# Rows turned later, their router product in the second value visit, their sums in the visit of step 8

## The chip, the cores and the metric

One core of a Trainium2 chip runs the whole program. The metric is the time of one execution on the device, in microseconds; several executions of a kernel are given by their median. The core has a matrix engine (TensorE, "PE" in the profile, its weight loads "PEld"), a vector engine (VectorE, "DVE"), an activation engine (ScalarE, "ACT"), a general one (GpSimd, "POOL"), and SyncE ("SP"), from whose queue nearly all transfers are issued. Each engine works through its own instructions in the order in which the program lists them. TensorE writes to PSUM alone; VectorE and ScalarE read from there.

## The reference, cut to what matters

Three stages, one after the other, all in float32:

```python
p_packed = sm_attn(p, k, v)                    # 8 batches x 8 heads, 32 packed queries over 576 keys
attn_out = sm_attn(q, p_packed, p_packed)      # 576 queries over the 32 packed rows
x = attn_out.transpose(0, 2, 1, 3).reshape(4608, 512)
h = x @ w_in;  x = (h * sigmoid(h)) @ w_out    # 512 -> 2048 -> 512
logits = x @ w_gate;  e_idx = argmax(logits, axis=1)          # 8 experts
gate_w = softmax(logits)[e_idx];  eom = sigmoid(x @ w_output_gate)[e_idx]
for e in range(8):                             # each row through its one expert
    out[mask] = gate_w * eom * (relu(x[mask] @ w1[e]) @ w2[e])
```

The router's logits (16 columns: 8 for the gate, 8 for the output gate) are needed for each of the 4608 rows before the rows can be sorted by expert.

## The kernel before, in words

**Batches and steps.** `batch(b)` runs for b = 0 to 7 (8 batches of 576 rows). Its loop over f, 16 passes, is called *steps* here. A step holds, in this order: `mm1` (12 products into the PSUM tile `ps_h`, which has one buffer and holds the hidden block f), `act` (ScalarE's tanh, then VectorE's multiplication that makes g; both read `ps_h`, so the next step's `mm1` waits for them), the side work of the first position (f, 0), the splitting of g into a high and a low half (ScalarE `ghi`, VectorE `glo`, and two small ones for the last 64 rows), whatever is in the list `late`, `mm2` of two steps ago (12 products, into four accumulators), and the side work of the second position (f, 1).

**Side work.** `extra_steps(b)` writes by hand which step and position each piece takes; pieces of one position run in the order in which they are entered. Three kinds are interleaved with batch b:
- the attention of batch b + 1, as `s1` to `s9`: `s1` scores of the packed queries (maxima on VectorE, then a copy `e` by ScalarE), `s2` their transposes, `s3` the products with the values, once for each of two halves r (step 5 for r = 0, step 7 for r = 1), which VectorE scales into `pp`; `s4` (step 8) transposes `pp` into `ppt`; `s5` scores of the queries, `s6` and `s7` their softmax, `s8` and `s9` (steps 11 and 14) its turn and its two halves;
- `step_m`, in every even step at the first position: it folds `ppt` into `w_in` (products, ScalarE's high half, VectorE's low half);
- the rows of batch b - 1, whose last `mm2` comes in step 1 of batch b.

**The rows.** A group has 4 blocks of 128 rows (after even batches) or 5 (after odd ones, with the rest of two batches). `regroup` (step 1) stores the rows to DRAM and loads them back in another order into `mid`; `row_x` turns one block within 32 by 32 squares on VectorE (line 296); `row_logits` multiplies with the router's weights, a fourth of the columns in each fourth of the partitions, and ScalarE copies the parts out; `row_sum` transposes the parts on TensorE, adds the fourths on VectorE, and goes on into `finish`: for each block a maximum and its index, then a few small operations. `finish` puts `pick` into `late`, which puts `weight` there a step later. `place` counts the rows of each expert with small products, and puts `put` into `late`, which computes each row's position and scatters the entries into the table `perm` by GpSimd, one call for each block.

**PSUM.** The accumulators take four banks, `ps_h` two. The other two are one tile "a" with one buffer: all of `s1` to `s5`, `step_m`, the rows and `place` use it in turn, and each new visit waits until the readers of the one before are done. `psum(b)` and `bank(...)` both hand it out.

In batch 7 there is no attention; its hook prepares the expert stage (copies and splits of expert weights, gathers of the first group's rows). `last_rows` and `experts` follow and use `row_logits`, `row_sum` and `place` for the last groups by themselves.

Of the kernel before, what the change touches and what calls it, by code (L numbers as in the profile page):

```python
# [21 lines left out]
DM = 512  # L22
# [13 lines left out]
NL = 2 * E8  # L36
# [48 lines left out]
class Kernel:  # L85
# [209 lines left out]
        xq, xt = [self.mid[:, g[n] + a * DM:g[n] + a * DM + DM] for n in ("xq", "xt")]  # L295
        self.nc.vector.transpose(out=xt.rearrange("p (t c j) -> p t c j", c=4, j=32), in_=xq.rearrange("p (t i c) -> p t c i", c=4, i=32))

    def row_logits(self, g, ps=None):
        n = g["n"]
        if ps is None:  # L300
            ps = self.bank("ps_rl")
        xt = self.mid[:, g["xt"]:g["xt"] + n * DM].rearrange("p (t c j) -> p c t j", c=4, j=32)
        if n == 1:
            xn = self.mid[:, g["xt"]:g["xt"] + DM]
            for c in range(4):
                self.nc.tensor.matmul(ps[:, 0, :NL], xn[:, c * 128:c * 128 + 128], self.wgt[:, c, :NL], start=(c == 0), stop=(c == 3))
            self.nc.vector.tensor_copy(out=g["lg"][:, 0, :], in_=ps[:, 0, :NL])
            self.finish(g)
            return
        for i, a in enumerate(range(0, n, 4)):  # L310
            m = min(n - a, 4)
            for c in range(4):
                self.nc.tensor.matmul(ps[32 * c:32 * c + 32, i, :m * 128], self.wgt[:, c, :], xt[:, c, 4 * a:4 * a + 4 * m, :], start=True, stop=True)
        part = self.mid[:, g["part"]:g["part"] + n * 128]
        self.nc.scalar.copy(out=part, in_=ps.rearrange("p a b -> p (a b)")[:, :n * 128])

    def row_sum(self, g):
        n, ps = g["n"], self.bank("ps_rs").rearrange("p a b -> p (a b)")
        for a in range(n):
            at = g["part"] + a * 128  # L320
            self.nc.tensor.transpose(ps[:, a * 128:a * 128 + 128], self.mid[:, at:at + 128], self.ident)
        self.nc.vector.tensor_reduce(out=g["lg"][:, :n, :], in_=ps[:, :n * 128].rearrange("p (a c m) -> p a m c", a=n, c=4)[:, :, :NL, :],
                                     axis=AX.X, op=ALU.add)
        self.finish(g)
# [107 lines left out]
    def extra_steps(self, b):  # L432
        sched = {}

        def at(f, pos, fn):
            sched.setdefault((f, pos), []).append(fn)

        if b + 1 < B:
            att = self.att_steps(b + 1)
            for f, pos, *step in ((0, 1, "s1", 0), (3, 1, "s1", 1), (4, 1, "s2", 0), (5, 1, "s3", 0), (6, 1, "s2", 1),  # L440
                                  (7, 1, "s3", 1), (8, 1, "s4"), (9, 1, "s5", 0), (10, 0, "s6", 0), (10, 1, "s7", 0),
                                  (11, 1, "s8", 0), (11, 1, "s9", 0), (12, 1, "s5", 1), (13, 0, "s6", 1), (13, 1, "s7", 1), (14, 1, "s8", 1), (14, 1, "s9", 1)):
                at(f, pos, att[tuple(step)])
            for f, what in ((0, "k1"), (3, "q0"), (5, "v1"), (9, "q1")):
                at(f, 1, lambda what=what: self.load_att(b + 1, what))
            at(14, 0, lambda: self.step_m(b + 1, 0))
        if b + 2 < B:
            for what in ("p", "k0", "v0"):
                at(13, 0, lambda what=what: self.load_att(b + 2, what))
        if b > 0:  # L450
            at(1, 1, lambda: self.regroup(self.group))
            for a in range(4 if b % 2 else 5):
                at(*((3, 0), (3, 1), (4, 0), (4, 1), (4, 1))[a], lambda a=a: self.row_x(self.group, a))
            if b + 1 == B:
                at(5, 1, lambda: self.row_logits(self.group))
            at(7, 0, lambda: self.row_sum(self.group))
            at(9, 0, lambda: self.place(self.group))
        for c in range(1, 8):
            at(2 * c - 2 + (b == 0 and (c == 1 or c % 2 == 0)), 0, lambda c=c: self.step_m(b, c))
        return sched  # L460
# [86 lines left out]
    def att_steps(self, b):  # L547
        nc, pa = self.nc, self.pa
# [35 lines left out]
        def s3(r):  # L584
            v = self.loads.pop((b, f"v{r}"))
            ps = self.psum(b)
            if r == 0 and b > 1:
                self.row_logits(self.group, ps)
            ps = ps[:, 1, 256:320]
            for ch in range(5):  # L590
                for c in range(4):
                    nc.tensor.matmul(ps[32 * c:32 * c + 32, :], a1[r][:, ch, 32 * c:32 * c + 32],
                                     v[:, ch, 64 * c:64 * c + 64], start=(ch == 0), stop=(ch == 4))
            nc.vector.tensor_scalar(out=self.pp[:, 64 * r:64 * r + 64], in0=ps,
                                    scalar1=st["sm"][:, 10 + r:11 + r], scalar2=None, op0=ALU.mult)

        def s4():
            ps = self.psum(b)
            nc.tensor.transpose(ps[:, 0, :128], self.pp, self.ident)
            ppt = self.p1.tile([128, 128], F32, tag="ppt", bufs=2, name="ppt")  # L600
            nc.scalar.copy(out=ppt, in_=ps[:, 0, :128])
            self.ppt[b] = ppt

        def grp(x):
            return x.rearrange("p a (t n) -> p (a t) n", n=NP)
# [34 lines left out]
        def s9(h):  # L640
# [3 lines left out]

        return {(f.__name__, *a): (lambda f=f, a=a: f(*a)) for f, a in
                [(f, (h,)) for f in (s1, s2, s3, s5, s6, s7, s8, s9) for h in range(2)] + [(s4, ())]}

    def step_m(self, b, c, split=False):
# [450 lines left out]
```

## Time and profile before

| | |
|---|---|
| median of 3 runs | 1237.77 us (1237.06 to 1238.42) |
| profiled execution | 1236.86 us, of which the span of instructions is 1235.0 |
| TensorE busy | 1171.0 us, 95% |
| its weight loads | 966.4 us, 78% |
| VectorE busy | 678.7 us, 55% |
| ScalarE busy | 467.4 us, 38% |
| GpSimd busy | 171.9 us, 14% |
| mean granted TensorE clock | 0.976 |
| DMA | 130.27 MB, mean 105 GB/s |

The span runs from the first instruction to the last; the time of the execution holds a little more around it. A matmul's end is modelled, so records of neighbours overlap, and a busy TensorE is not one at its peak. The granted clock is a share of the full 2.4 GHz; 0.5 is 1.2 GHz. In the rows below "[5.38 <-ACT e L561]" says that the engine stood idle for 5.38 us in front of this instruction, and that the instruction that ended the idle time was ScalarE's at line 561 on tile `e`.

### The profile page before, as it was taken

The page shows a single profiled execution, that of the slowest core. Times are in us where ns is not written, and L with a number is a line of the kernel's source. Part 1 is how long each engine was busy: PE and PEld are TensorE (multiplying, and loading weights), DVE is VectorE, ACT ScalarE, POOL GpSimd, SP SyncE. Part 2 cuts the span into 40 slices and gives each one's busy share as a digit, 9 for nine tenths or more (in the row PEclk, how much of TensorE's full clock was granted, in tenths as well). Part 3 has the DMA queues.
Part 4 walks back from the last instruction along what each step waited for, and adds up shares of the span by engine and source line. Part 5 has one row for each costly group of instructions (what it writes and reads, how often), then busy time and mean ns, then how long its engine had stood idle before and what let it go on. Part 6 is the DMA issues. An engine that isn't in the chain of part 4 may idle for free. (4 is left out here: it accounts for less than half of the span.)

```text
span 1235.0 us, 20793 instructions
## 1 busy us (share of the span) xinstructions
PE 1171.0 (95%) x8307; PEld 966.4 (78%) x8307; DVE 678.7 (55%) x1355; ACT 467.4 (38%) x913; POOL 171.9 (14%) x177
## 2 busy tenths in 40 slices
PE   7796989999989999989999989999999999999996
PEld 3575768778768777768777878879899998999985
DVE  6888646545646545645645746454454454544531
ACT  2343433433443433443433434323443434434331
POOL 0234201000001000000000121013312113111011
PEclk8699989999999999999999999999999999999999
DMA  8564230231240231131141052116645546455221
GB/s 321 177 208 171 95 77 24 95 71 44 62 107 25 76 91 44 45 104 45 61 105 35 9 144 71 69 45 205 188 110 180 150 132 197 115 176 162 70 74 41
DMA packets 105290, 130.27 MB, mean 105 GB/s; under 512 B 13888, under 2 KB 80640, under 8 KB 104928
## 3 DMA queue, kind: packets, MB, share of 16 engines
q1 hardware_dynamic: 97888, 108.76, 30.0%
q0 software_dynamic: 7296, 20.09, 5.0%
q8 instruction: 67, 1.10, 0.4%
q14 instruction: 39, 0.32, 0.1%
HBM read 99.12 MB, written 21.57 MB: 98 GB/s over the span
## 5 line engine op out<-in xcount | busy, mean ns | idle before, releaser
L728 PE MATMUL acc<-wo,ghi 128*128 128x512 f32 x1024 | 322.6, 397 | 0.0
L728 PEld LDWEIGHTS acc<-wo,ghi 128*128 128x128 f32 x1024 | 195.9, 191 | 38.8
L1013 PE MATMUL pu<-xt,w 128*128 128x256 f32 (+1 forms) x1536 | 214.5, 295 | 0.1
L677 PE MATMUL ps_h<-a,m_hi 128*128 128x288 f32 x1024 | 213.1, 301 | 0.6 <-DVE a L643 0.6
L1013 PEld LDWEIGHTS pu<-xt,w 128*128 128x128 f32 x1536 | 208.6, 189 | 5.5 <-PE ps_r L782 0.2
L728 PE MATMUL acc<-wo,glo 128*128 128x512 f32 x512 | 211.3, 413 | 0.7 <-DVE glo L697 0.7
L1038 PE MATMUL py<-w,xt 128*128 128x512 f32 x768 | 188.2, 394 | 0.0
L687 DVE SCALAR_TENSOR_TENSOR g<-g,ps_h 128x576 f32<-128x576 f32 x128 | 95.9, 750 | 148.8 <-ACT g L686 148.7
L677 PE MATMUL ps_h<-a,m_lo 128*128 128x288 f32 x512 | 161.3, 315 | 13.6 <-DVE g L687 6.8
L677 PEld LDWEIGHTS ps_h<-a,m_hi 128*128 128x128 f32 x1024 | 169.1, 194 | 3.0 <-DVE a L643 0.9
L1038 PEld LDWEIGHTS py<-w,xt 128*128 128x128 f32 x768 | 144.2, 188 | 33.4
L686 ACT ACTIVATE g<-ps_h 128x576 f32<-128x576 f32 x128 | 83.5, 652 | 165.0 <-PE ps_h L677 161.5
L1019 DVE SCALAR_TENSOR_TENSOR xt<-pu,xt 128x512 fp32r<-128x512 f32 (+1 forms) x128 | 58.7, 459 | 145.0 <-ACT xt L1018 145.0
L728 PEld LDWEIGHTS acc<-wo,glo 128*128 128x128 f32 x512 | 98.0, 191 | 45.0 <-issue 26.7
L1018 ACT ACTIVATE xt<-pu 128x512 fp32r<-128x512 f32 (+1 forms) x128 | 52.8, 412 | 211.3 <-PE pu L1013 162.3
L677 PEld LDWEIGHTS ps_h<-a,m_lo 128*128 128x128 f32 x512 | 99.0, 193 | 35.8 <-issue 12.1
L799 POOL DMA_INDIRECT perm<-pay,dsti x36 | 36.0, 1000 | 601.4 <-DVE dsti L797 476.2
L697 DVE TENSOR_TENSOR glo<-g,ghi 128x512 fp32r<-128x512 f32 x128 | 90.6, 708 | 41.4 <-ACT ghi L692 37.6
L692 ACT CAST ghi<-g 128x512 fp32r<-128x512 f32 x128 | 79.6, 622 | 78.0 <-DVE g L687 77.7
L975 DVE TENSOR_TENSOR w<-raw,w 128x1024 fp32r<-128x1024 f32 x64 | 78.4, 1226 | 40.9 <-ACT w L974 38.6
L974 ACT CAST w<-raw 128x1024 fp32r<-128x1024 f32 x64 | 67.0, 1048 | 0.0
L545 PE MATMUL ps_m<-w_in,ppt 64*32 64x256 f32 x1008 | 44.8, 403 | 21.9 <-ACT e L561 19.8
(184 smaller groups left out, 1046.3 us busy)
## 6 DMA issues: line engine op xcount, KB each, us to landing
raw<-in_w SPq DMA_DIRECT2D x64, 512.0 KB
att_v<-in_v SPq DMA_DIRECT2D x15, 640.0 KB
att_k<-in_k SPq DMA_DIRECT2D x15, 576.0 KB
stg<-in_w_in SPq DMA_DIRECT2D x16, 512.0 KB
stg<-in_w_out SPq DMA_DIRECT2D x16, 512.0 KB
xr<-xr SPq DMA_DIRECT2D x32, 256.0 KB
att_q<-in_q SPq DMA_DIRECT2D x14, 576.0 KB
mid<-xr SPq DMA_DIRECT2D x28, 256.0 KB
```

The costliest lines, as they stand in the source:

```text
L677: nc.tensor.matmul(ps[:, hf, :288], lw[:, qd, fs], rx[:, qd, ts], start=(i == 0), stop=(i == 5))
L686: nc.scalar.activation(out=g2, in_=ps[:, :, :288], func=AF.Tanh, scale=0.5)
L687: nc.vector.scalar_tensor_tensor(out=g2, in0=g2, scalar=1.0, in1=ps[:, :, :288], op0=ALU.add, op1=ALU.mult)
L692: self.nc.scalar.copy(out=hi, in_=self.graw[:, :512])
L697: self.nc.vector.tensor_tensor(out=lo, in0=self.graw[:, :512], in1=self.ghi.bitcast(F32), op=ALU.subtract)
L728: self.nc.tensor.matmul(acc, l, r, start=(first and i == 0), stop=(last and i == 2))
L974: nc.scalar.copy(out=hi, in_=raw)
L975: nc.vector.tensor_tensor(out=lo, in0=raw, in1=hi.bitcast(F32), op=ALU.subtract)
L1013: nc.tensor.matmul(ps[:, hf, :m], w[:, k, r, fs], xt[:, l, k, ts], start=(i == 0), stop=(i == 11))
L1018: nc.scalar.activation(out=hi, in_=src, func=AF.Relu)
L1019: nc.vector.scalar_tensor_tensor(out=lo, in0=src, scalar=0.0, in1=hi.bitcast(F32), op0=ALU.max, op1=ALU.subtract)
L1038: nc.tensor.matmul(self.acc[j], hl[:, l + j * 128:l + j * 128 + 128], w[:, r], start=(first and i == 0), stop=(last and i == 2))
```

## The change

Three edits. The `row_x` of a group go from steps 3 and 4 to steps 5, 6 and 7. The router's products go from the visit of `s3(0)` in step 5 into that of `s3(1)` in step 7, and ScalarE's copy of the parts is now listed behind the products of the values, not ahead of them. The transposes and sums of `row_sum` go from a visit of their own at the head of step 7 into the visit of `s4` in step 8: `pp` is transposed to other columns of the tile, the parts' transposes follow, then ScalarE's copy `ppt`, then VectorE's sum and `finish`. `place` goes from step 9 to step 11. In batch 7, which has no `s3` and no `s4`, the products and the sums stay visits of their own, in steps 7 and 8. `row_logits` and `row_sum` are cut into two functions each for that; what is computed stays the same.

```diff
@@ -295,30 +295,43 @@
         xq, xt = [self.mid[:, g[n] + a * DM:g[n] + a * DM + DM] for n in ("xq", "xt")]
         self.nc.vector.transpose(out=xt.rearrange("p (t c j) -> p t c j", c=4, j=32), in_=xq.rearrange("p (t i c) -> p t c i", c=4, i=32))
 
-    def row_logits(self, g, ps=None):
+    def row_logits(self, g):
+        n, ps = g["n"], self.bank("ps_rl")
+        if n > 1:
+            self.row_products(g, ps)
+            self.row_part(g, ps)
+            return
+        xn = self.mid[:, g["xt"]:g["xt"] + DM]
+        for c in range(4):
+            self.nc.tensor.matmul(ps[:, 0, :NL], xn[:, c * 128:c * 128 + 128], self.wgt[:, c, :NL], start=(c == 0), stop=(c == 3))
+        self.nc.vector.tensor_copy(out=g["lg"][:, 0, :], in_=ps[:, 0, :NL])
+        self.finish(g)
+
+    def row_products(self, g, ps):
         n = g["n"]
-        if ps is None:
-            ps = self.bank("ps_rl")
         xt = self.mid[:, g["xt"]:g["xt"] + n * DM].rearrange("p (t c j) -> p c t j", c=4, j=32)
-        if n == 1:
-            xn = self.mid[:, g["xt"]:g["xt"] + DM]
-            for c in range(4):
-                self.nc.tensor.matmul(ps[:, 0, :NL], xn[:, c * 128:c * 128 + 128], self.wgt[:, c, :NL], start=(c == 0), stop=(c == 3))
-            self.nc.vector.tensor_copy(out=g["lg"][:, 0, :], in_=ps[:, 0, :NL])
-            self.finish(g)
-            return
         for i, a in enumerate(range(0, n, 4)):
             m = min(n - a, 4)
             for c in range(4):
                 self.nc.tensor.matmul(ps[32 * c:32 * c + 32, i, :m * 128], self.wgt[:, c, :], xt[:, c, 4 * a:4 * a + 4 * m, :], start=True, stop=True)
-        part = self.mid[:, g["part"]:g["part"] + n * 128]
-        self.nc.scalar.copy(out=part, in_=ps.rearrange("p a b -> p (a b)")[:, :n * 128])
+
+    def row_part(self, g, ps):
+        n = g["n"]
+        self.nc.scalar.copy(out=self.mid[:, g["part"]:g["part"] + n * 128], in_=ps.rearrange("p a b -> p (a b)")[:, :n * 128])
 
     def row_sum(self, g):
-        n, ps = g["n"], self.bank("ps_rs").rearrange("p a b -> p (a b)")
-        for a in range(n):
+        ps = self.bank("ps_rs")
+        self.row_turns(g, ps)
+        self.row_add(g, ps)
+
+    def row_turns(self, g, ps):
+        ps = ps.rearrange("p a b -> p (a b)")
+        for a in range(g["n"]):
             at = g["part"] + a * 128
             self.nc.tensor.transpose(ps[:, a * 128:a * 128 + 128], self.mid[:, at:at + 128], self.ident)
+
+    def row_add(self, g, ps):
+        n, ps = g["n"], ps.rearrange("p a b -> p (a b)")
         self.nc.vector.tensor_reduce(out=g["lg"][:, :n, :], in_=ps[:, :n * 128].rearrange("p (a c m) -> p a m c", a=n, c=4)[:, :, :NL, :],
                                      axis=AX.X, op=ALU.add)
         self.finish(g)
@@ -450,11 +463,11 @@
         if b > 0:
             at(1, 1, lambda: self.regroup(self.group))
             for a in range(4 if b % 2 else 5):
-                at(*((3, 0), (3, 1), (4, 0), (4, 1), (4, 1))[a], lambda a=a: self.row_x(self.group, a))
+                at(*((5, 0), (5, 1), (6, 0), (6, 1), (7, 0))[a], lambda a=a: self.row_x(self.group, a))
             if b + 1 == B:
-                at(5, 1, lambda: self.row_logits(self.group))
-            at(7, 0, lambda: self.row_sum(self.group))
-            at(9, 0, lambda: self.place(self.group))
+                at(7, 1, lambda: self.row_logits(self.group))
+                at(8, 1, lambda: self.row_sum(self.group))
+            at(11, 0, lambda: self.place(self.group))
         for c in range(1, 8):
             at(2 * c - 2 + (b == 0 and (c == 1 or c % 2 == 0)), 0, lambda c=c: self.step_m(b, c))
         return sched
@@ -584,22 +597,30 @@
         def s3(r):
             v = self.loads.pop((b, f"v{r}"))
             ps = self.psum(b)
-            if r == 0 and b > 1:
-                self.row_logits(self.group, ps)
-            ps = ps[:, 1, 256:320]
+            rows = r == 1 and b > 1
+            if rows:
+                self.row_products(self.group, ps)
+            both, ps = ps, ps[:, 1, 256:320]
             for ch in range(5):
                 for c in range(4):
                     nc.tensor.matmul(ps[32 * c:32 * c + 32, :], a1[r][:, ch, 32 * c:32 * c + 32],
                                      v[:, ch, 64 * c:64 * c + 64], start=(ch == 0), stop=(ch == 4))
+            if rows:
+                self.row_part(self.group, both)
             nc.vector.tensor_scalar(out=self.pp[:, 64 * r:64 * r + 64], in0=ps,
                                     scalar1=st["sm"][:, 10 + r:11 + r], scalar2=None, op0=ALU.mult)
 
         def s4():
-            ps = self.psum(b)
-            nc.tensor.transpose(ps[:, 0, :128], self.pp, self.ident)
+            both = self.psum(b)
+            ps = both[:, 1, 128:256]
+            nc.tensor.transpose(ps, self.pp, self.ident)
+            if b > 1:
+                self.row_turns(self.group, both)
             ppt = self.p1.tile([128, 128], F32, tag="ppt", bufs=2, name="ppt")
-            nc.scalar.copy(out=ppt, in_=ps[:, 0, :128])
+            nc.scalar.copy(out=ppt, in_=ps)
             self.ppt[b] = ppt
+            if b > 1:
+                self.row_add(self.group, both)
 
         def grp(x):
             return x.rearrange("p a (t n) -> p (a t) n", n=NP)
```

## Rows read from the trace of the kernel before

**Rows 1.** The waits, whole trace: who waited, for whom: us in total, times, longest.

```profile
ACT e L561 <- DVE sm L560: 60.8, 16, 7.5
...
DVE mid L296 <- DMA mid<-xr: 24.7, 7, 5.9
```

**Rows 2.** Timeline of TensorE, steps 4 and 5: start us, length us, instruction, idle before.

```profile
167.52 1.11 PE L545 MATMUL ps_m<-w_in,ppt 64*32 64x256 f32 x16 [5.38 <-ACT e L561]
...
266.24 0.67 PE L545 MATMUL ps_m<-w_in,ppt 64*32 64x256 f32 x16 [0.90 <-ACT e L561]
...
355.14 0.67 PE L545 MATMUL ps_m<-w_in,ppt 64*32 64x256 f32 x16 [3.46 <-ACT e L561]
...
453.71 0.67 PE L545 MATMUL ps_m<-w_in,ppt 64*32 64x256 f32 x16 [0.87 <-ACT e L561]
...
543.58 1.11 PE L545 MATMUL ps_m<-w_in,ppt 64*32 64x256 f32 x16 [4.42 <-ACT e L561]
...
642.22 0.67 PE L545 MATMUL ps_m<-w_in,ppt 64*32 64x256 f32 x16 [1.03 <-ACT e L561]
...
732.55 0.40 PE L677 MATMUL ps_h<-a,m_lo 128*128 128x288 f32 x1 [3.10 <-DVE g L687]
```

**Rows 3.** Timeline of VectorE, batch 1, steps 3 to 5.

```profile
164.34 1.08 DVE L296 STREAM_TRANSPOSE mid<-mid 128x512 f32<-128x512 f32 x1 [5.84 <-DMA mid<-xr]
...
175.84 0.75 DVE L687 SCALAR_TENSOR_TENSOR g<-g,ps_h 128x576 f32<-128x576 f32 x1 [2.94 <-ACT g L686]
```

**Rows 4.** Windows: length; busy PE, PEld, DVE, ACT, POOL; granted clock; DMA share, GB/s.

```profile
164.00:168.00 4.00, 0.48 (x16) 0.23 (x16) 3.59 (x7) 1.17 (x2) 0.00 (x0) 0.60 0.30 98
168.00:172.00 4.00, 4.00 (x25) 2.77 (x10) 3.62 (x9) 2.80 (x8) 0.00 (x0) 0.55 0.00 0
355.20:359.20 4.00, 4.00 (x25) 2.82 (x26) 3.94 (x9) 3.34 (x8) 0.00 (x0) 0.59 0.02 4
543.60:547.60 4.00, 4.00 (x24) 2.61 (x25) 3.70 (x7) 3.26 (x8) 0.00 (x0) 0.57 0.00 0
```

**Rows 5.** Tile `mid`: who waited for its instructions (us in total, times).

```profile
  PE ps_s L592: 4.6, 6
```

**Rows 6.** Timeline of ScalarE and TensorE, batch 1, step 5.

```profile
178.93 0.59 ACT L315 COPY mid<-ps_s 128x512 f32<-128x512 f32 x1 [1.53 <-PE ps_s L313]
...
179.56 0.77 PE L592 MATMUL ps_s<-att_v,a1t 128*32 128x64 f32 x40 [0.71 <-ACT mid L315]
```

**Rows 7.** Timelines of VectorE and TensorE, batch 2, steps 7 to 10.

```profile
286.48 0.48 DVE L322 TENSOR_REDUCE lg<-ps_rs 128x80 f32<-128x320 f32 x1
...
289.16 0.69 DVE L697 TENSOR_TENSOR glo<-g,ghi 128x512 fp32r<-128x512 f32 x1
...
293.78 0.19 DVE L766 TENSOR_REDUCE rt<-sh 128x5 f32<-128x40 f32 x1
...
294.23 0.27 PE L599 MATMUL ps_s<-cst,pp 128*128 128x128 f32 x1
...
295.93 0.66 PE L782 MATMUL ps_r<-oh,tri 128*128 128x8 bf16 x20
...
296.87 0.76 DVE L687 SCALAR_TENSOR_TENSOR g<-g,ps_h 128x576 f32<-128x576 f32 x1 [2.27 <-ACT g L686]
...
299.06 0.19 DVE L793 SCALAR_TENSOR_TENSOR dst<-cst,dst 128x40 f32<-128x40 f32 x1
...
300.00 0.40 PE L677 MATMUL ps_h<-a,m_lo 128*128 128x288 f32 x1
```

**Rows 8.** Timelines of VectorE and TensorE, batch 2, steps 11 and 12.

```profile
308.59 0.75 DVE L687 SCALAR_TENSOR_TENSOR g<-g,ps_h 128x576 f32<-128x576 f32 x1
...
309.60 0.29 PE L677 MATMUL ps_h<-a,m_lo 128*128 128x288 f32 x1
...
313.62 0.68 DVE L659 TENSOR_TENSOR m_lo<-ps_m,m_hi 128x512 fp32r<-128x512 f32 x1
...
314.85 0.72 PE L545 MATMUL ps_s<-att_q,ppt 64*32 64x288 f32 x16
```

## The prediction

> **What bounds the kernel now.** I read the engine shares first. TensorE is busy 95% of the span and no other engine over 55%, so a change pays only where TensorE stands still or runs at the lower clock, in the stretch that the diff touches: batches 1 to 7, from about 140 to 790 us. Next the waits, whole trace: VectorE waited seven times, 24.7 us in all, for the transfer that brings the rows back for `row_x` (line 296) [rows 1]. Then the timeline of TensorE in steps 4 and 5 of each batch (a step is one pass of the loop over f in `batch`): in batches 1 to 6 its longest stand ends at the product `step_m` of step 4 (line 545), released by ScalarE's copy of the scores `e` out of PSUM; in batch 7 it ends at a product of step 5 (line 677), released by VectorE. The seven stands are 5.38, 0.90, 3.46, 0.87, 4.42, 1.03 and 3.10 us, 19.16 in sum [rows 2].
>
> They are one cause. `row_x(0)` is issued in step 3. In batch 1 VectorE stood 5.84 us in front of it until the transfer had landed at 164.34 [rows 3]; queued behind it were the low half of g, the maxima of `s1(1)` and, behind those on ScalarE, the copy of `e`. That copy releases the one PSUM tile "a", which `step_m` needs. In batch 7, without attention, the row was late for the next activation instead.
>
> The windows show a second part. After the three longest stands TensorE was granted 0.60, 0.55, 0.59 and 0.57 of its clock over 4 us each, so it ran at 1.2 GHz, the lower level, for (1 - share) x 4 / 0.5 us, and loses half of what it works in that time: 0.24 us (it worked 0.48 of that window, all of it at the low level) + 1.8 + 1.64 + 1.72 = 5.4 us [rows 4].
>
> The Trainium skill ("Perfetto Trace Analysis", Identifying the Most-Contended Engine) says that matmul busy time is no good measure of how near TensorE is to its limit. The trace agrees: from 168 to 172 us it is busy 4.00 of 4.00 us at 0.55 of the clock. By busy time alone 19.2 us could be had here; with the clock it is 24.6.
>
> The second wait that the diff names is in step 5: the router's products (line 313) sit in the PSUM tile of `s3(0)`, ScalarE copies them out, and only then do the products of the values (line 592) start: six times, 4.6 us of standing in all, 0.71 of them in batch 1 [rows 5, 6].
>
> **The change, part by part.** Durations come from the profiled execution, 1236.86 us (span 1235.0 and 1.86 around it); the median of the runs is 1237.77, 0.91 more.
>
> *Row turns two steps later* (`row_x` from steps 3 and 4 to 5, 6 and 7). The transfers (`regroup`, step 1) are issued by SP as before and behind the same instructions, so they land at the same time. In batch 1 the activation of step 5, behind which `row_x(0)` now stands, ran at 175.84 [rows 3]; without the 7.4 us lost in step 4 (5.38 and 2.0 by the clock) that is 168.4, and the rows are there at 164.34: 4 us to spare. Two steps of batch 1 without those 7.4 us are about 10 us, twice the longest wait. So 19.16 + 5.4 = **24.6 us go**. What is late next in step 4 is ScalarE's copy of `e` itself; with VectorE free it ends about when TensorE wants the tile. In steps 5 to 7 each turn adds 1.1 us to VectorE. In step 6 it stands ahead of the low half of `step_m`, and that releases the tile for `s2(1)`: as it stood in step 4 before, where the same order left no stand of its own. I cost that at zero, with up to 0.2 us a batch the other way.
>
> *Products in the visit of the second values* (step 7), ScalarE's copy behind both products. The 4.6 us go; as the two products now follow each other without a pause, their recorded ends overlap too. Bounds: 4.6 (the gaps alone) and 6.4 (0.3 us of overlap more each time, an estimate: half of a product's recorded length or less). I take **5.0**. New wait: VectorE's scaling of `pp` stands behind ScalarE's copy, as reads of one PSUM tile go one after the other here (the copy of `e` waited for the maxima of the same tile sixteen times [rows 1]). Queued behind it is the activation of step 8. The copy took 0.59 us [rows 6] and the scaling is shorter, together about 1 us, while TensorE has the first product of step 8, some 1.7 us (294.23 to 295.93 in step 9 [rows 7]), before it wants the tile. Nothing.
>
> *Sums in the tile of step 8.* The transposes of `row_turns` cost TensorE what they cost in step 7. `row_add` waits for the copy of `ppt`, and behind it stands `finish`. With five blocks sum and `finish` held VectorE 2.68 us, from 286.48 to 289.16 [rows 7]. Now they fall at the end of step 8, ahead of the activation of step 9. Counted in batch 2: the transpose of `s4` started at 294.23; with five more, the copy and 2.68, `finish` ends at about 298.0. The activation of step 9 ran at 296.87 and would now be ready at 297.3 (behind the transposes' 0.45), so it is 0.7 us late and ends at 298.75. TensorE went on to step 10 at 300.00 and will at 299.95, the transposes in and `place`'s 0.5 out [rows 7]. Cover 1.2 us, more with four blocks: nothing.
>
> *What `finish` leaves for later steps.* `weight` (five instructions, the first, of 0.19, at 293.78) moves from step 8 to 10, `place` from 9 to 11, and `put` (four, the first at 299.06) to step 11 [rows 7], each some 0.75 us of VectorE (an estimate: five or four instructions of up to 0.19, their overlaps and pauses). Steps 10 to 12 were the fullest. Batch 2: the activation of step 11 started at 308.59, late already, and ended 0.26 us before TensorE went on at 309.60 [rows 8]. `weight` pushes it by 0.75, to 310.1. `place` gives TensorE 0.5 us more in that step (20 small matmuls, recorded over 0.66 us with their overlap [rows 7]), so TensorE wants it at 310.1: a stand of 0 to 0.1. Then `put` stands ahead of `y`, so `y`, the cast behind it and the activation of step 12 come 0.75 + 0.75 = 1.5 later. The low half of step 12's `step_m` would start at 315.1 instead of 313.62 and end at 315.8. It releases the tile for the scores of `s5(1)`, which started at 314.85 [rows 8] and are now wanted at 315.36: **0.5 us of standing, a new wait**. Batches 1 to 6: 6 x 0.5 = **3.1 us back**, with the 0.1. Bounds: 0, and 12 us if each delay counts without cover (2 us x 6).
>
> The moved scatter on GpSimd, the last instructions that `put` issues, has steps 12 to 15 for itself; its table is first read in step 1 of batch 7. No cost.
>
> Sum: 24.6 + 5.0 - 3.1 = 26.5. 1236.86 - 26.5 = 1210.4 for the profiled execution; as a median 0.9 more: **1211 us**.
>
> **The rivals.**
> 1. *No give-back.* `s5(1)` gets its tile in time and the products overlap fully: 24.6 + 6.4 = 31, so 1207. For it: chains of 1.5 us rest on modelled ends. Against: in steps 11 and 12 VectorE already ran without a pause.
> 2. *Thinner cover.* Sum, `weight` and `put` each cost TensorE something, 1.2 to 2 us a batch in place of 0.5, or the turns in steps 6 and 7 hold up the products: 24.6 + 5 - 7 to 12 = 17.6 to 22.6, so 1215 to 1220. For it: in step 6 the turn and the low half leave TensorE little slack. Against: 1.2 us of cover in step 9.
> 3. *Slower, by `finish`.* One mechanism: VectorE works in order, and at the end of step 8 `finish` (2.68) comes ahead of an activation without which TensorE can't overwrite its PSUM tile. If it ran without any cover, with the two small groups behind it (1.5), TensorE would stand over 3.5 us, and after a stand of 3.46 the clock fell to the lower level and cost 1.6 [rows 2, 4]. That is 5.2 x 6 = 31 us against 29.6 won: about 1239. It decides from 4.9 us a batch. Against: TensorE has some 2.6 us of the second product to do before it needs the activation.
> 4. *The wait only moves with the turns*: the transfer lands after step 5 too. Only the 4.6 of step 5 would go: 1233. For it: in batch 1 the rows were 5.84 us late. Against: two steps give 9 us or more.
>
> **How the numbers follow.** Forecast (1208.5 to 1214.5) 0.60; rival 1 0.15; rival 2 0.18; rival 3 0.04; rival 4 0.03. The range: below, rival 1 with 2 us for the overlaps, 1205; above, rival 2 with a little over its bound, 1221. About 0.1 is left outside. A difference of 0.2%, 2.5 us, is what can be told from no change. Faster takes the forecast and rivals 1, 2 and 4 less a remainder: 0.94; same 0.02; slower 0.04.
>
> **What would show it.** Right: no VectorE wait for `mid` at line 296 (now 24.7 us); no stand over 0.3 us at `step_m` of step 4; a granted clock of 1.00 through batches 1 to 7; line 592 without a wait for ScalarE's copy; a new stand of about half a microsecond at `s5(1)` in step 12, released by the low half of `step_m`, in each of batches 1 to 6; the stretch after batch 7 as long as before. Wrong: `mid` still waited for in step 5 (rival 4); stands at step 10's first product released by VectorE (rival 3); stands in steps 6 or 7 released by the turns (rival 2); or the expert stage longer, which the sum leaves unchanged.

## The result and the profile after

The changed kernel takes 1209.06 us (median of 4 runs, 1207.84 to 1209.56) against 1237.88 for the kernel before on the same chip (median of 4): a ratio of 0.9766, 95% interval 0.9749 to 0.9783. The profiled execution took 1209.23 us (before: 1236.86), 27.6 less.

The page of the changed kernel: the span, and the busy time of the engines with its share and their instructions.

```profile
span 1207.4 us, 20785 instructions
...
PE 1163.2 (96%) x8305; PEld 959.9 (80%) x8307; DVE 679.5 (56%) x1355; ACT 467.4 (39%) x913; POOL 171.1 (14%) x177
```

VectorE, ScalarE and GpSimd work as long as before, within 0.8 us. TensorE's busy time fell by 7.8 us though its work is the same. Summed from its rows, 5.7 of that lie in batches 1 to 7, where the prediction had found 5.4 lost to the lower clock, and 2.1 in batch 0, whose code did not change. The time that TensorE stood in batches 1 to 7 fell from 23.75 us to 1.97.

The first wait of [rows 1] in the changed kernel (who waited, for whom: us in total, times, longest), shorter than it was, and a new one:

```profile
ACT e L574 <- DVE sm L573: 43.6, 16, 5.2
...
DVE pp L610 <- ACT mid L320: 12.0, 6, 2.1
```

The second wait of [rows 1], for the returning rows, is gone. All that the changed kernel did at line 296 (count: shortest, median and longest ns, first and last start; then what VectorE waited for in front of it, an empty list):

```profile
L296 DVE STREAM_TRANSPOSE mid<-mid x31: 1080/1100/1104, 169.0 to 714.9; 128x512 f32<-128x512 f32 x31
...
its engine sat idle before it (us, times) until:
```

Windows of the changed kernel over batches 1 to 6 and over batch 7 up to its last step (columns as in [rows 4]; the seventh value, after the five engines, is the granted clock):

```profile
140.00:680.00 540.00, 538.04 (x4342) 426.82 (x4341) 310.52 (x712) 220.71 (x463) 27.11 (x30) 1.00 0.25 67
681.10:753.80 72.70, 72.70 (x500) 59.67 (x498) 41.49 (x101) 30.12 (x63) 11.66 (x13) 1.00 0.36 95
```

TensorE now works 538 of 540 us at full clock; what [rows 4] showed after the stands is nowhere in this stretch.

Where the time went can be read step by step, as the distance from the first product of `mm1` in one step to that in the next. Worked out from all TensorE rows of both kernels (us after, and change):

```
step        batch 1       batch 2       batch 3       batch 4       batch 5       batch 6       batch 7
 4        5.74 -7.26    5.73 -0.94    5.74 -5.08    5.74 -0.91    5.74 -6.04    5.74 -1.07    5.11 -3.26
 5        5.20 -1.77    5.20 -2.10    5.20 -1.77    5.20 -2.10    5.20 -1.78    5.20 -2.10    4.33 -1.21
 6        5.75 +0.06    5.74  0.00    5.75  0.00    5.75  0.00    5.75 +0.06    5.74  0.00    5.11 -0.16
 7        6.06 +0.41    6.28 +0.54    6.06 +0.41    6.28 +0.54    6.06 +0.41    6.28 +0.54    5.41 +0.63
 8        5.75 +0.44    5.85 +0.54    5.75 +0.44    5.85 +0.54    5.75 +0.44    5.85 +0.54    5.64 +0.53
 9        5.15 -0.46    5.17 -0.58    5.15 -0.46    5.17 -0.58    5.15 -0.46    5.17 -0.58    4.41 -0.42
11        4.80 +0.48    4.93 +0.60    4.85 +0.52    4.93 +0.59    4.85 +0.52    4.93 +0.60    4.77 +0.45
12        6.36 +0.51    6.28 +0.39    6.36 +0.47    6.36 +0.47    6.36 +0.46    6.35 +0.50    5.11  0.00
```

All other steps of these batches agree within 0.05 us. From the start of batch 1 to the end of step 14 of batch 7 it is 614.18 us after 641.67, so 27.49 less; from there to the end 453.57 after 453.50. Batch 0, whose code is the same, takes a microsecond more or less from one execution to the next (in the ten profiled executions of this study batch 1 began between 138.4 and 140.6 us; in the two of the changed kernel at 139.6 and 138.4), so the experiments below are read from the steps of batches 1 to 7, and their totals with that in mind.

Step 7 of batch 1 in the changed kernel answers to [rows 6] (start us, length us, engine, line, operation):

```profile
181.25 1.07 PE L316 MATMUL ps_s<-mid,wgt 128*32 128x512 f32 x8
...
182.13 0.74 PE L606 MATMUL ps_s<-att_v,a1t 128*32 128x64 f32 x40
...
182.94 0.59 ACT L320 COPY mid<-ps_s 128x512 f32<-128x512 f32 x1 [2.03 <-PE ps_s L606]
...
183.56 0.28 DVE L610 TENSOR_SCALAR pp<-ps_s,sm 128x64 f32<-128x64 f32 x1 [1.94 <-ACT mid L320]
```

The products of the values follow the router's without a pause and even start 0.19 us before those end in the record (181.25 + 1.07 = 182.32). ScalarE's copy and VectorE's scaling come behind both.

Steps 8 to 10 of batch 2 in the changed kernel answer to [rows 7]:

```profile
283.90 0.27 PE L616 MATMUL ps_s<-cst,pp 128*128 128x128 f32 x1
284.01 0.71 PE L331 MATMUL ps_s<-cst,mid 128*128 128x128 f32 x5
...
285.05 0.49 DVE L335 TENSOR_REDUCE lg<-ps_s 128x80 f32<-128x320 f32 x1 [1.52 <-ACT ppt L620]
...
285.58 0.17 DVE L773 MAX8 mx<-lg 128x8 f32<-128x8 f32 x1
...
287.42 0.17 DVE L774 CAST rt<-ix 128x5 f32<-128x5 uint32 x1
...
287.74 0.75 DVE L708 SCALAR_TENSOR_TENSOR g<-g,ps_h 128x576 f32<-128x576 f32 x1
...
289.64 0.40 PE L698 MATMUL ps_h<-a,m_lo 128*128 128x288 f32 x1
...
290.25 0.84 DVE L637 STREAM_TRANSPOSE x<-ps_s 128x288 f32<-128x288 f32 x2
...
291.43 0.66 PE L558 MATMUL ps_m<-w_in,ppt 64*32 64x256 f32 x16
```

Sum and `finish` hold VectorE from 285.05 to 287.74, 2.69 us, and the activation of step 9 stands right behind them. It ends at 288.49, 1.15 us before TensorE begins step 10. A second margin shows in the last two rows: the transposes of `x` out of the tile "a" end at 291.09, and `step_m` of step 10, which takes that tile, starts 0.34 us later. With four blocks the trace has 1.56 and 0.75 us at these two places.

Steps 11 and 12 of batch 2 in the changed kernel answer to [rows 8]:

```profile
298.94 0.75 DVE L708 SCALAR_TENSOR_TENSOR g<-g,ps_h 128x576 f32<-128x576 f32 x1
...
299.84 0.30 PE L698 MATMUL ps_h<-a,m_lo 128*128 128x288 f32 x1
...
301.12 0.19 DVE L814 SCALAR_TENSOR_TENSOR dst<-cst,dst 128x40 f32<-128x40 f32 x1
...
301.89 0.77 DVE L657 STREAM_TRANSPOSE y<-x 128x576 f32<-128x576 f32 x1
...
304.07 0.74 DVE L708 SCALAR_TENSOR_TENSOR g<-g,ps_h 128x576 f32<-128x576 f32 x1
304.74 0.68 DVE L680 TENSOR_TENSOR m_lo<-ps_m,m_hi 128x512 fp32r<-128x512 f32 x1
...
305.47 0.72 PE L558 MATMUL ps_s<-att_q,ppt 64*32 64x288 f32 x16 [0.35 <-DVE m_lo L680]
```

The four instructions of `put` (301.12 to 301.89) stand ahead of `y`; `m_lo` ends at 305.42, and the scores of `s5(1)` start 0.05 later, after a stand of 0.35 us. The same stand is there in batches 1 to 6, 0.27 to 0.37 us; before, none was at this place.

### The profile page after: what moved, and what is told of

Its sections match the earlier page's. It is cut to its first block, busy times and chain, and to the rows that moved or that the text cites. A ratio compares the mean times of both kernels' runs of the same rounds, so it can differ in the third digit from the quotient of the medians.

```text
span 1207.4 us, 20785 instructions
## 1 busy us (share of the span) xinstructions
PE 1163.2 (96%) x8305; PEld 959.9 (80%) x8307; DVE 679.5 (56%) x1355; ACT 467.4 (39%) x913; POOL 171.1 (14%) x177
## 5 line engine op out<-in xcount | busy, mean ns | idle before, releaser
L749 PE MATMUL acc<-wo,ghi 128*128 128x512 f32 x1024 | 319.1, 393 | 0.0
L749 PEld LDWEIGHTS acc<-wo,ghi 128*128 128x128 f32 x1024 | 193.2, 189 | 37.8
L749 PE MATMUL acc<-wo,glo 128*128 128x512 f32 x512 | 208.5, 407 | 0.8 <-DVE glo L718 0.8
```

Source lines behind the costliest of these rows:

```text
L749: self.nc.tensor.matmul(acc, l, r, start=(first and i == 0), stop=(last and i == 2))
```

## The experiments

Each kernel is the changed one with one edit. Theory: the changed kernel wins by the turns' positions (24.6 us) and the joined products (some 5), and gives 3 back in steps 11 and 12 by `weight` and `put`.

**Turns at their old places.** One part of the change undone, the rest left in.

```diff
-                at(*((5, 0), (5, 1), (6, 0), (6, 1), (7, 0))[a], lambda a=a: self.row_x(self.group, a))
+                at(*((3, 0), (3, 1), (4, 0), (4, 1), (4, 1))[a], lambda a=a: self.row_x(self.group, a))
```

> The changed kernel (1209.1 us) with the row turns back in steps 3 and 4; products, sums and place stay where the change put them. Theory: the wait of VectorE for the rows is the whole of what step 4 gave (24.6 us in the two traces: 19.2 of standing and 5.4 of lower clock), so it comes back entirely, the stands at step_m of step 4 with it, and the granted clock falls again after the long ones: 1233 to 1235 us. Rival: part of the gain in step 4 comes from the products and sums having left steps 5 and 7, which lets VectorE run ahead; then the turns alone bring back 12 to 18 us: 1221 to 1227.

1236.35 us (1235.12 to 1237.88, 10 runs), ratio to the kernel before 0.999 (0.9979 to 1.0001). The rival is out: with the turns back nearly the whole gain is gone. But the time is 1.4 us above the theory's upper end. Its VectorE wait at line 296, of the kernel with the turns at their old places:

```profile
DVE mid L296 <- DMA mid<-xr: 23.8, 7, 5.9
```

The stands, three of seven, in TensorE's timeline of the same kernel:

```profile
166.13 1.11 PE L558 MATMUL ps_m<-w_in,ppt 64*32 64x256 f32 x16 [5.41 <-ACT e L574]
...
352.99 1.11 PE L558 MATMUL ps_m<-w_in,ppt 64*32 64x256 f32 x16 [3.58 <-ACT e L574]
...
729.29 0.40 PE L698 MATMUL ps_h<-a,m_lo 128*128 128x288 f32 x1 [2.91 <-DVE g L708]
```

All seven are there, each within 0.31 us of its counterpart in [rows 2], 18.3 us in all where the kernel before had 19.16. The clock behind three of them is not the same. Windows of the same kernel, batches 3, 5 and 7:

```profile
352.80:356.80 4.00, 3.81 (x23) 2.42 (x24) 3.86 (x6) 3.29 (x9) 0.00 (x0) 0.50 0.00 0
356.80:360.80 4.00, 4.00 (x23) 3.53 (x22) 1.33 (x3) 0.92 (x4) 0.00 (x0) 0.82 0.02 4
540.50:544.50 4.00, 3.71 (x22) 2.38 (x23) 3.94 (x6) 3.29 (x8) 0.00 (x0) 0.50 0.00 0
544.50:548.50 4.00, 4.00 (x23) 3.48 (x22) 1.34 (x3) 1.01 (x4) 0.00 (x0) 0.82 0.00 0
729.00:733.00 4.00, 3.71 (x16) 3.42 (x17) 4.00 (x7) 1.42 (x3) 3.04 (x4) 0.66 0.48 131
733.00:737.00 4.00, 4.00 (x22) 3.32 (x21) 1.11 (x3) 0.77 (x2) 2.62 (x4) 0.91 0.64 171
```

And the kernel before, behind its stand of 3.10 us in batch 7:

```profile
732.50:736.50 4.00, 3.95 (x22) 3.58 (x23) 3.97 (x6) 1.42 (x3) 3.12 (x4) 1.00 0.42 122
```

In batch 3, half of the 3.81 us and half of the 1.44 us (0.18 x 4 / 0.5) that TensorE worked at 1.2 GHz are lost, 2.6 us, against 1.7 in the kernel before; step 4 of this batch is 0.91 longer than before. Batch 5 is alike, 2.6 against 1.7, though its stand is 0.31 shorter than before. In batch 7 it loses up to (0.34 + 0.09) x 4 = 1.7 us, where the kernel before lost nothing; step 5 is 1.70 longer than in the changed kernel. So the waits are one sum, and the clock behind them another that differs between the two traces: in the steps, undoing the turns costs 27.2 us and not 24.6, of which 18.3 are standing and 8.9 the clock.

The other steps of this kernel differ from those of the kernel before as the changed kernel's do, within 0.05 us: the joined products and the give-back are there, 2.8 us shorter together. The clock took nearly all of that back: batches 1 to 7 are only 0.28 us shorter than before in the traces. By the medians the kernel is 1.35 us shorter (95% interval 2.6 shorter to 0.1 longer). As these medians, of ten and thirteen runs, fall short of the 2.8 too, one odd execution is not the likely cause. Whether the extra loss of clock belongs to this kernel or only to some of its executions is not shown.

**Turns one step later instead of two.**

```diff
-                at(*((5, 0), (5, 1), (6, 0), (6, 1), (7, 0))[a], lambda a=a: self.row_x(self.group, a))
+                at(*((4, 0), (4, 1), (5, 0), (5, 1), (6, 0))[a], lambda a=a: self.row_x(self.group, a))
```

> The changed kernel with the row turns one step earlier, in steps 4 to 6, in place of 5 to 7. Theory: the rows land 24.5 us after the start of batch 1 and 23.8 after that of batch 7, and the activation of step 4 ends 23.9 and 22.3 us after it, so VectorE waits 0.7 us in batch 1, 1.5 in batch 7 and not at all in the others; TensorE loses 0.7 us at the transposes of step 4 in batch 1 and next to nothing in batch 7: 1209 to 1211 us. Rival: each step of delay takes away its own share of the wait, so one step is worth about half of the 24.6: 1219 to 1223 us.

1210.01 us (1208.97 to 1210.16), ratio 0.9772 (0.9755 to 0.979): the theory. Only step 4 of batch 1 is longer, by 0.74 us. The rows are there 24.6 us after the start of batch 1, as in the kernel before (24.5), so the transfer itself did not become faster. The wait that is left in this kernel:

```profile
DVE mid L296 <- DMA mid<-xr: 1.8, 2, 1.1
```

VectorE waits 0.77 us in batch 1 and 1.05 in batch 7, where TensorE loses nothing by it. So one step is enough for TensorE in all batches but one, and the second step is the margin. A transfer that is 5.9 us late is nearly met by a single step of delay, as a step takes 5.1 to 5.7 us here.

**The copy ahead of the products.** In step 7, `row_part` goes back between the router's products and those of the values.

```diff
                 self.row_products(self.group, ps)
-            both, ps = ps, ps[:, 1, 256:320]
+                self.row_part(self.group, ps)
+            ps = ps[:, 1, 256:320]
...
-            if rows:
-                self.row_part(self.group, both)
```

> The changed kernel with ScalarE's copy of the router's parts listed ahead of the products of the values again, in step 7 as it is now. Theory: the order of the copy is what steps 5, 7 and 8 gained together (0.92 us with four blocks, 1.02 with five, 5.8 in all), so step 7 gets 0.9 to 1.0 us longer in batches 1 to 6 and line 607 (values) waits for the copy again: 1214.5 to 1215.5 us. Rival: the gain is from the products' new place beside the later turns and the order is worth nothing, as the copy would then hold up VectorE's scaling less: 1209 us.

1215.08 us (1213.55 to 1215.18), ratio 0.9812 (0.9794 to 0.983): the theory. Step 7 is longer by 0.91 us (four blocks) and 1.02 (five), three times each; with four, step 8 is 0.06 shorter. That is 5.6 us in all, nearly the whole of what the joined products gave. TensorE in step 7 of batch 1 of this kernel:

```profile
183.40 0.77 PE L607 MATMUL ps_s<-att_v,a1t 128*32 128x64 f32 x40 [0.70 <-ACT mid L320]
```

The stand is the 0.71 of [rows 6], and 0.2 us of overlap goes with it. With four blocks the router's products fill the first bank of the tile alone and the products of the values go into the second; they wait all the same. The Trainium skill ("PSUM — Partial Sum Buffer", PSUM bank collisions raise a hardware error) asks for semaphores by bank and quadrant; by that rule no wait is needed here with four blocks, and three of the six stands would be absent. The trace has all six, 0.70 or 0.71 us with four blocks and 0.81 with five: the order kept here is one of whole tiles.

**Sums in a visit of their own**, behind `s4` in the same step.

```diff
-            if b > 1:
-                self.row_turns(self.group, both)
...
             if b > 1:
-                self.row_add(self.group, both)
+                self.row_sum(self.group)
```

> The changed kernel with the sums of step 8 in a visit of their own behind the visit of s4, in place of sharing its tile. Theory: the transposes of the parts then wait for ScalarE's copy of ppt (0.27 us and the way there and back), a stand of 0.4 to 0.6 us in each of batches 1 to 6, while finish comes out some 0.3 us later, which its cover of 1.15 us takes: 1211.5 to 1213 us. Rival: finish is nearer to its limit than the cover says, and the first product of step 10 waits too: over 1214 us.

1212.21 us (1211.68 to 1212.97), ratio 0.9792 (0.9775 to 0.981): the theory. Step 8 is 0.58 us longer in each of six batches, 9 and 10 are not. TensorE in step 8 of batch 1 of this kernel:

```profile
188.56 0.66 PE L331 MATMUL ps_rs<-cst,mid 128*128 128x128 f32 x4 [0.36 <-ACT ppt L618]
```

A second visit to the tile "a" has to wait for the reader of the first, and the joined visit avoids that. It is a cost avoided and not one taken away: the kernel before had no stand at its separate visit in step 7. The run says little on the cover of `finish`: the sum comes 0.28 us later than in the changed kernel, counted from the start of the batch, but TensorE's next steps come 0.58 later, so the cover grew (1.45 us with five blocks).

**`place` in step 15**, in batches 1 to 6: takes TensorE's small products and the four instructions of `put` out of steps 11 and 12, but leaves `weight` in step 10.

```diff
-            at(11, 0, lambda: self.place(self.group))
+            at(11 if b + 1 == B else 15, 0, lambda: self.place(self.group))
```

> The changed kernel with place in step 15 in place of 11 in batches 1 to 6; weight stays in step 10. Theory: two groups of small VectorE work make the new wait of step 12, weight (step 10) and put (behind place); with put gone the tile for the scores of step 12 comes in time, but place no longer gives TensorE 0.5 us in step 11, so the activation that weight delays is now 0.5 us late there: steps 11, 12 and 15 together stay as long (15.5 us with four blocks), the stand only moves from the scores of step 12 to its first product, released by g: 1208.5 to 1209.5 us, no change. Rival: put alone makes the wait, and its going takes 0.47 us from each of six batches: 1206 to 1206.5 us.

1210.91 us (1209.94 to 1211.36), ratio 0.9778 (0.9764 to 0.9791), where the changed kernel itself took 1208.5 on the same chip. The theory's mechanism is what the trace shows. TensorE in steps 11 and 12 of batch 2 of this kernel:

```profile
300.79 0.40 PE L698 MATMUL ps_h<-a,m_lo 128*128 128x288 f32 x1 [0.34 <-DVE g L708]
...
306.16 0.72 PE L558 MATMUL ps_s<-att_q,ppt 64*32 64x288 f32 x16
```

The stand at `s5(1)` is gone and one of the same size stands at the first product of step 12 instead: without `place`'s products TensorE comes there earlier, and the activation, pushed by `weight`, is late for it. Over steps 11, 12 and 15 that is +0.11 us with four blocks and +0.2 with five, 0.93 in all; of the rest of the 2.4 us the trace shows nothing in batches 1 to 7 (batch 1 began at 140.6 us, in the second trace of the changed kernel at 138.4). As a time it missed its expectation by 1.4 us, as a mechanism not. Its five runs all lie above the five of the changed kernel, so the rest is more than one slow start, and why it is there stays open.

**`weight` and `place` both in step 15**, in batches 1 to 6.

```diff
-            at(11, 0, lambda: self.place(self.group))
+            if b + 1 < B:
+                at(15, 0, lambda: self.group["weight"]())
+            at(11 if b + 1 == B else 15, 0, lambda: self.place(self.group))
...
-            self.late.append(weight)
+            if g["b"] < B - 2:
+                g["weight"] = weight
+            else:
+                self.late.append(weight)
```

> The changed kernel with both weight and place in step 15 in batches 1 to 6, where VectorE has room. Theory: with both gone from steps 10 and 11 these have their durations of before without place (5.27, 4.33 and 5.85 to 5.89 us for steps 10 to 12) and step 15 takes place's 0.5 us: the 2.8 us of give-back go, 1206 to 1206.6 us. Rival: the stand of step 12 comes from the order of y, its cast and the activation alone and stays: 1209 us; or step 15 or the next batch's first steps wait in turn: 1208 us or more.

1206.26 us (1205.07 to 1206.91), ratio 0.9743 (0.9729 to 0.9756): the theory, and 2.2 us less than the changed kernel on the same chip (1208.5), so this version beats both. Steps 11, 12 and 15 together are shorter by 0.44 to 0.59 us in each of six batches, 3.14 in all. VectorE and TensorE in steps 11 and 12 of batch 2 of this kernel:

```profile
297.32 0.75 DVE L710 SCALAR_TENSOR_TENSOR g<-g,ps_h 128x576 f32<-128x576 f32 x1
...
298.34 0.29 PE L700 MATMUL ps_h<-a,m_lo 128*128 128x288 f32 x1
...
302.35 0.68 DVE L682 TENSOR_TENSOR m_lo<-ps_m,m_hi 128x512 fp32r<-128x512 f32 x1
...
303.53 0.72 PE L560 MATMUL ps_s<-att_q,ppt 64*32 64x288 f32 x16
```

The activation ends 0.27 us before TensorE wants it and `m_lo` 0.50 before `s5(1)`. In the changed kernel's rows above the two are 0.15 and 0.05; in its other batches the first is only 0.05 to 0.09.

**The loop over the maxima twice**, in the groups of batches 0 to 5: VectorE gets 1.7 us more ahead of the activation of step 9 (five blocks; 0.34 us a block) or 1.4 (four). The result is the same.

```diff
-        for r in range(n):
+        for r in [*range(n)] * (2 if g["b"] < B - 2 else 1):
```

> The changed kernel with the maxima and their indices of finish taken twice in batches 1 to 6, which adds 1.5 (four blocks) or 1.84 us (five) to VectorE ahead of the activation of step 9 and leaves the result as it is. Theory: the trace shows that activation end 1.15 us before TensorE goes on (five blocks), so some 0.75 us of the 1.84 come out at the first product of step 10, and as much again at step_m of step 10, whose tile waits for the turns of the scores behind the activation: 1.0 to 1.6 us in batches 2, 4 and 6 and up to 0.7 in 1, 3 and 5: 1212 to 1216 us. Rival (finish has no cover): all of it comes out, 10 us: 1219 us or more. Other rival (finish is fully hidden): 1209 us.

1214.96 us (1214.38 to 1215.01), ratio 0.9812 (0.9796 to 0.9827): the theory's range. With five blocks step 9 is longer by 0.61 us, step 10 by 0.91, step 12 shorter by 0.28; with four, 0, 0.75 and 0.2. That is 5.1 us in all, of 6.5 by the medians. TensorE in batch 2 of this kernel:

```profile
291.44 0.40 PE L698 MATMUL ps_h<-a,m_lo 128*128 128x288 f32 x1 [0.54 <-DVE g L708]
...
294.14 0.67 PE L558 MATMUL ps_m<-w_in,ppt 64*32 64x256 f32 x16 [0.83 <-DVE x L637]
```

The first stand is 1.70 of added work less the cover of 1.15: 0.55, measured 0.54. The second is what is left of the added work behind that stand, 1.70 - 0.54 = 1.16, less the 0.34 us ahead of `step_m` in step 10: 0.82, measured 0.83. So both margins read in the changed kernel are real, and the one that decides is the smaller: with four blocks, where 1.4 us don't reach the first (1.56), the second already costs 0.75. The steps grew a little more than the stands, because even a product that is waited for starts 0.05 us (the first) or 0.15 (`step_m`) behind the end of what releases it. Less these, the margins are 1.1 and 0.19 us with five blocks and 1.5 and 0.60 with four, and the growth of the steps follows from them within 0.03.

**The changed kernel once more**, on the chip of the last three.

> The changed kernel unaltered, beside the three others on the same chip: 1208 to 1210 us by every theory.

1208.5 us (1208.02 to 1209.42), ratio 0.9762 (0.9749 to 0.9776).

## Why the prediction was right, step by step

Forecast 1211, measured 1209.06; 26.5 us less forecast for the profiled execution, 27.6 measured. By its terms:

- *What bounds the kernel.* Right. The gain lies where TensorE stood or ran slowly, and 1.2 us of it in products that now overlap: VectorE, ScalarE and GpSimd have the busy time they had.
- *Turns two steps later, -24.6.* Step 4 of the seven batches sums to -24.56. They agree to 0.1 us because both are read from the same trace of the kernel before: all that this trace lost there went. Another trace could have given another sum, so the size is partly luck: with the turns put back, the standing was 18.3 where it had been 19.2, but the clock took 8.9 in place of 5.4, so 27.2 in all. The first turn now starts at 169.0, where 168.4 was forecast as its earliest time, and waits for nothing; with one step instead of two, 0.74 us is left.
- *Turns in steps 6 and 7, zero, up to 0.2 a batch.* Step 6 gives +0.12 over batches 1 to 6.
- *Products in one visit, -5.0 between 4.6 and 6.4.* This is the term that was mis-sized most: steps 5, 7 and 8 give 0.92 with four blocks and 1.02 with five, 5.82 in all. The gaps of 4.6 were right; the overlap that comes back with them is 0.2 us each time, of which the forecast took 0.07.
- *New wait of the scaling for the copy, nothing.* VectorE waited 12.0 us for it in all, and TensorE none: the scaling ended at 183.84, and no stand is at step 8.
- *Sum and `finish` ahead of the activation, covered by 1.2 us.* Measured 1.15, and no stand in step 10. What the prediction did not see is the second margin, 0.34 us at `step_m` of step 10, of which 0.19 can be used. It cost nothing here, but rival 3 would have begun to cost earlier than its working had it: it needs not 1.2 us of delay but 0.2.
- *`place` from step 9 to 11, 0 to 0.1 a batch.* Step 9 lost 0.46 or 0.58, step 11 gained 0.48 to 0.60: +0.19 net in six batches.
- *New stand at `s5(1)`, 0.5 a batch.* Step 12 grew by 0.39 to 0.51, 2.80 in all, at the place and by the releaser that were named. With the 0.19 that is 2.99 for a forecast of 3.1, and moving both groups away gave 3.14 back. The recorded stand is shorter, 0.27 to 0.37. As the ends of matmuls are modelled, the price is read from the step's length.
- *Batch 7 and the stretch after.* Steps 5 to 14 of batch 7 gave 0.21 that was in no term. The expert stage came out unchanged, as said.

Sum of batches 1 to 7: -24.56 - 5.82 + 2.99 + 0.12 - 0.21 = -27.48, for 27.49 measured. Of the 1.0 us by which this exceeds the forecast, 0.8 is the overlap of the products. Rival 1 had nearly the right overlap (5.82 of its 6.4 came) but no give-back, which is there; rival 2's thinner cover and rival 3's stand at step 10 are absent, until the maxima run twice; rival 4 is excluded by the empty list at line 296.

## What to carry over

When VectorE waits for a transfer in the middle of its queue, price the wait by the stand of TensorE behind it and by the time it then works at the lower clock, and keep the two apart: in two traces with the same waits the first came to 19.2 and 18.3 us, the second to 5.4 and 8.9. Before work is pushed to a later step, list every consumer behind it in the queue and the slack of each; the first one named was not the one with the least slack here (1.15 against 0.34 us in the rows). Small groups of VectorE instructions that a move displaces have a price where the queue is full, though not all that they take: some 1.5 us a batch (the forecast's estimate) made step 12 about 0.5 us longer. In a step with room they cost nothing: from steps 10 and 11 to 15 they were worth another 2.2 us.

## What the runs showed of the hardware beyond that

- What the clock did behind a stand differed between two traces. With the turns at their old places it was granted 0.66 and 0.91 over the 8 us after a stand of 2.91 us in batch 7; in the kernel before, after one of 3.10 at the same place, 1.00. After stands of 3.58 and 4.11 us in batches 3 and 5 the first had 0.50 and then 0.82 over 4 us each, and 0.83 already over the 4 us before; the second, after 3.46 and 4.42 us, had 0.59 and 0.57, then 0.98 and 1.00. What makes the difference was not tried, and stays open.
- The products of the values and the router's, both in a fourth of the columns, overlap by 0.19 us when they follow each other; separating them costs that as well as the gap.
